# A Nystrom attention with an MLP on one core: another stationary operand for the iteration, late stores, and loads in parts

## The chip, the cores and the metric

One core of one Trainium2 chip. The metric is the time of one execution in device microseconds (us). Every kernel here was profiled once and timed in several rounds beside the kernel before on the same chip. Engines: PE is TensorE, DVE is VectorE, ACT is ScalarE, POOL is GpSimd, SP is the engine whose queue issues nearly all DMAs.

## The reference, cut to what matters

```python
# q, k, v: 8 batches, 8 heads, 576 rows, 64 columns; m = 32 landmarks (means of 18 rows)
A  = softmax(q    @ k_lm.T)          # 576 x 32 per head
Bm = softmax(q_lm @ k_lm.T)          # 32 x 32
C  = softmax(q_lm @ k.T)             # 32 x 576
Z  = Bm.T / (norm1(Bm) * norminf(Bm))
for _ in range(6):
    Z = 2 * Z - Z @ Bm @ Z           # inverse of Bm by iteration
attn = A @ Z @ C @ v
# then, over 4608 rows of 512: layer norm, MLP 512 -> 2048 -> 512 with relu, residual
```

## The kernel before: the parts that the change touches

Heads are handled four at a time, one above the other on 128 partitions; such a group of four is a unit (W units at once: two for one batch, four for two). The kernel does not iterate on Z. It holds E = (scaled Bm times its transpose) in the first 32 columns of a tile st and X, which starts as C @ v, in the other 64, and takes both from one product: E becomes 2E - EE and X becomes 2X - EX. Names that come up later: psn is that product in PSUM, ebd (fbd after the change) E (F) as a block-diagonal stationary operand; bmbd and zcbd are block-diagonal operands of the end of an attention, rcv the reciprocals that scale X; nat, asum and s are POOL's casts and sums for the landmarks; psh is the first product of the MLP and ot an output block.

```python
    def diagonal(name, src, W, mask):       # 32x32 blocks of four heads -> block diagonal 128x128
        t = asm.tile([P, W, 4, LM], FP16, name=name, tag=name, bufs=1)
        dve.tensor_tensor(out=t[:], in0=src[:, :, None, :].broadcast_to([P, W, 4, LM]),
                          in1=mask, op=ALU.mult)
        return t
    ...
        for it in range(6):
            lo = 0 if it < 5 else LM
            psn = p1([P, W, LM + D], "psn")
            for w in range(W):
                MM(psn[:, w, lo:], ebd[:, w, :, :].rearrange("p a l -> p (a l)"), st[:, w, lo:])
            stn = asm.tile([P, W, LM + D], FP16, name="st", tag="st")
            dve.scalar_tensor_tensor(out=stn[:, :, lo:], in0=st[:, :, lo:], scalar=2.0,
                                           in1=psn[:, :, lo:], op0=ALU.mult,
                                           op1=ALU.subtract)
            st = stn
            if it < 5:
                ebd = diagonal("ebd", st[:, :, 0:LM], W, masks(W))
            ...
```

The MLP is a stream of TensorE work, cut into 36 row blocks in nine groups; after each step of an attention, `fill(n)` puts n of its matmuls into the program. TensorE's order is thereby fixed. A group of the MLP needs the normalized rows (xn, by POOL) of four blocks, turned by DMA transposes (xnT). Batch 0 runs first with nothing to fill in but idle matmuls, then batch 1, batch 2, batches 3 and 4, 5 and 6, 7.

The softmax here doesn't subtract the row's maximum and nothing guards it: scores larger than these inputs give would overflow.

## Time and profile before

| | before |
|---|---|
| time, median of the first 3 runs | 329.13 us (328.23 to 330.18) |
| span of the profiled run | 327.9 us |
| TensorE busy | 314.7 us, 96% |
| first psh (start of the MLP) | 25.95 us |
| first psh of the fourth MLP group | 141.71 us |
| from there to the end | 186.2 us |

The prediction below shows the page's shares and slices. Two groups of instructions belong beside them; the columns are line, engine, operation, what it writes and reads with partitions and elements, count, then busy us, mean ns of one, and idle time of the engine before them with its cause.

```profile
L68 DVE SCALAR_TENSOR_TENSOR st<-st,psn 128x192 f16<-128x192 f16 (+3 forms) x36 | 14.2, 395 | 17.6 <-PE psn L74 17.4
L68 DVE TENSOR_TENSOR ebd<-st,mask 128x256 f16<-128x256 f16 (+1 forms) x30 | 20.7, 690 | 1.0
```

These are the two VectorE operations of each step. The reader is to see that the step is short, some 1 us of VectorE, and that ebd is the dearer half.

### The profile page before, as it was taken

The numbers are of one execution on the slowest core, as the hardware profiler recorded it, in microseconds if no ns is written. First come the engines' busy times: TensorE is split into PE (matmuls) and PEld (weight loads), VectorE is DVE, ScalarE is ACT, GpSimd is POOL, SyncE is SP. The second block draws the span as 40 slices with busy tenths as digits, with TensorE's granted clock in tenths as the row PEclk, the third lists the DMA queues.
The fourth block names the chain that finished last, engine by engine and source line by source line (L and its number), as shares of the span: only waits on it lengthen the run. The fifth ranks groups of instructions, "written<-read, shape, count | busy, mean of one in ns | idle before, by whom it ended". The sixth has DMA issues, their size and how long they took to land.

```text
span 327.9 us, 8249 instructions
## 1 busy us (share of the span) xinstructions
PE 314.7 (96%) x3409; PEld 162.3 (50%) x3409; DVE 175.7 (54%) x395; ACT 152.7 (47%) x307; POOL 153.3 (47%) x241
## 2 busy tenths in 40 slices
PE   8889999999999999989999999999999999999995
PEld 8547864553445444435544445454444444444444
DVE  3668769779964797953237668722566120010012
ACT  3546762749960661957204672454046107305600
POOL 3389979999999999999800034100014000000000
PEclk9999999999999999999999999999999999999998
DMA  7999999898797864695022103330242126032023
GB/s 278 394 356 365 366 402 303 297 345 239 241 195 231 234 169 127 156 290 102 4 68 66 34 20 76 82 50 2 64 104 26 32 64 98 0 72 60 0 49 79
DMA packets 36397, 50.34 MB, mean 154 GB/s; under 512 B 17796, under 2 KB 22152, under 8 KB 36360
## 3 DMA queue, kind: packets, MB, share of 16 engines
q1 hardware_dynamic: 36200, 49.69, 52.7%
q8 instruction: 26, 0.43, 0.5%
q10 hardware_dynamic: 160, 0.13, 0.2%
q14 instruction: 11, 0.09, 0.1%
HBM read 36.70 MB, written 9.44 MB: 141 GB/s over the span
## 4 chain that ended last, share of the span: by engine, by line
PE 56%; POOL 22%; DMA 7%; issue 2%; ACT 2%; DVE 1%; SPq 0%; POOLq 0%
PE psh L74 26%; PE pso L74 25%; POOL asum L68 11%; POOL nat L68 6%; POOL natv L68 3%; DMA stg<-in_q_dram 3%; POOL xn L68 2%; DMA w2stg<-in_moe_w_ch_dram 2%; POOL s L68 1%; PE psy L74 1%; PE pscv L74 1%; DMA stg<-in_v_dram 1%; DMA stg<-in_k_dram 1%; DMA xnT<-xn 1%; ACT xn L68 1%
## 5 line engine op out<-in xcount | busy, mean ns | idle before, releaser
L74 PE MATMUL psh<-xnT,w 128*128 128x512 f16 (+1 forms) x640 | 133.7, 358 | 1.4 <-DMA xnT<-xn 1.4
L74 PE MATMUL pso<-w,hT 128*128 128x512 f16 (+1 forms) x592 | 132.9, 374 | 0.0
L68 ACT ACTIVATE hT<-psh 128x512 f16<-128x512 f32 x144 | 84.9, 597 | 97.6 <-PE psh L74 97.4
L74 PEld LDWEIGHTS <-w 128*128 128x128 f16 x640 | 59.5, 98 | 56.7 <-issue 3.1
L74 PEld LDWEIGHTS <-hT 128*128 128x128 f16 x592 | 56.1, 98 | 57.2 <-issue 0.8
L68 DVE SCALAR_TENSOR_TENSOR ot<-pso,rstd,xblk 128x512 f32<-128x512 f32 (+1 forms) x37 | 27.1, 732 | 77.6 <-PE pso L74 77.4
L68 POOL CAST nat<-stg 128x1152 f16<-128x1152 f32 x28 | 32.5, 1167 | 3.4 <-DMA stg<-in_k_dram 1.7
L68 POOL TENSOR_TENSOR asum<-asum 128x256 f32<-128x256 f32 (+2 forms) x54 | 28.4, 527 | 4.2
L68 DVE TENSOR_TENSOR xblk<-psy,rcpd 128x512 f32<-128x512 f32 (+1 forms) x40 | 27.6, 691 | 1.8 <-POOL w L68 0.2
L68 POOL TENSOR_TENSOR asum<-nat 128x576 f32<-128x576 f16 x18 | 23.4, 1299 | 1.5
L68 POOL TENSOR_SCALAR xn<-xblk,mvg 128x512 f16<-128x512 f32 x14 | 9.6, 694 | 30.9 <-ACT junk L68 30.9
L68 DVE SCALAR_TENSOR_TENSOR st<-st,psn 128x192 f16<-128x192 f16 (+3 forms) x36 | 14.2, 395 | 17.6 <-PE psn L74 17.4
L68 POOL CAST natv<-stg 128x1152 f16<-128x1152 f32 (+1 forms) x16 | 17.6, 1119 | 9.6 <-DMA stg<-in_v_dram 9.6
L68 POOL TENSOR_SCALAR negm<-mvg 128x1 f32<-128x1 f32 x14 | 2.7, 191 | 40.5 <-DVE mvg L68 35.9
L68 DVE TENSOR_TENSOR ebd<-st,mask 128x256 f16<-128x256 f16 (+1 forms) x30 | 20.7, 690 | 1.0
L68 DVE STREAM_TRANSPOSE xT<-nat 128x576 uint32<-128x576 uint32 x24 | 18.2, 760 | 2.2 <-POOL nat L68 2.2
L74 PE MATMUL psy<-zcbd,ea 128*128 128x260 f16 (+1 forms) x80 | 15.9, 276 | 1.0 <-DVE xblk L68 0.4
L68 ACT ACTIVATE ea<-psea 128x576 f16<-128x576 f32 x12 | 7.2, 648 | 16.5 <-PE psea L74 16.5
L74 PE MATMUL idle<-zeros 128*128 128x128 f16 (+2 forms) x82 | 13.4, 312 | 1.1 <-DVE eps_ln L172 1.1
L74 PEld LDWEIGHTS <-ea 128*128 128x128 f16 (+1 forms) x80 | 7.1, 100 | 12.2 <-issue 3.5
L68 ACT ACTIVATE junk<-xblk 128x512 f16<-128x512 f32 x14 | 8.8, 625 | 9.4 <-DVE xblk L68 9.2
L68 DVE BATCH_NORM_STATS2 st<-xblk 128x6 f32<-128x512 f32 x18 | 12.4, 688 | 0.5
(115 smaller groups left out, 263.0 us busy)
## 6 DMA issues: line engine op xcount, KB each, us to landing
stg<-in_q_dram SPq DMA_DIRECT2D x16, 576.0 KB, 6.0
stg<-in_k_dram SPq DMA_DIRECT2D x16, 576.0 KB, 5.7
out_dram<-ot SPq DMA_DIRECT2D x70, 128.0 KB, 2.4
stg<-in_v_dram SPq DMA_DIRECT2D x10, 576.0 KB, 6.4
w1stg<-in_moe_w_ch_dram SPq DMA_DIRECT2D x16, 256.0 KB, 6.0
w2stg<-in_moe_w_ch_dram SPq DMA_DIRECT2D x16, 256.0 KB, 5.2
stg<-in_v_dram SPq DMA_DIRECT2D x12, 288.0 KB, 5.5
xnT<-xn SPq DMA_TRANSPOSE x28, 3.3
```

The source lines that it names most:

```text
L68: return lambda *args, **kw: keep(getattr(self.engine, op)(*args, **kw))
L74: keep(nc.tensor.matmul(o, l, r, start=start, stop=stop, tile_position=(rb, cb), skip_group_check=(skip or cb != 0)))
```

## The change

Its intent: shorten a step. With F = 2 - E as stationary operand, F times (E, X) is already the next (E, X), so VectorE has only to copy psn to st, and the next F can be taken straight from psn, without reading st. Off-diagonal blocks of fbd stay 0 for good, so only the four diagonal blocks are written, one op each. Beside it: stores of the output are put into the queue one step later, behind the loads and transposes of the step; the last loads of batch 0's k and v come in two parts; fewer idle matmuls there; bmbd is built before the iteration.

```diff
+    def two_less(e, W):
+        for h in range(4):
+            rows = ds(32 * h, 32)
+            dve.scalar_tensor_tensor(
+                out=fbd[rows, 0:W, h, :], in0=e[rows, :, :], scalar=-1.0,
+                in1=twos[rows, None, :].broadcast_to([32, W, LM]), op0=ALU.mult, op1=ALU.add)
+
+    def newton(st, psn, W, it):
+        if it < 5:
+            dve.tensor_copy(out=st[:], in_=psn[:])
+            two_less(psn[:, :, 0:LM], W)
+        else:
+            dve.tensor_copy(out=st[:, :, LM:], in_=psn[:, :, LM:])
 ...
-        ebd = diagonal("ebd", st[:, :, 0:LM], W, masks(W))
+        two_less(st[:, :, 0:LM], W)
 ...
-                MM(psn[:, w, lo:], ebd[:, w, :, :].rearrange("p a l -> p (a l)"), st[:, w, lo:])
+                MM(psn[:, w, lo:], fbd[:, w, :, :].rearrange("p a l -> p (a l)"), st[:, w, lo:])
-            dve.scalar_tensor_tensor(out=stn[:, :, lo:], in0=st[:, :, lo:], scalar=2.0, ...)
+            newton(stn, psn, W, it)
-            if it < 5:
-                ebd = diagonal("ebd", st[:, :, 0:LM], W, masks(W))
 ...
+        bmbd = asm.tile(...)          # now before the iteration
 ...
-                store(j, ot)
+                if at_end:
+                    store(j, ot)
+                else:
+                    to_store.append((j, ot))
 ...
+    def work(n):
+        k = len(to_store)
+        fill(n)
+        settle()
+        for _ in range(k):
+            store(*to_store.pop(0))
 ...   (k and v of batch 0 in parts, two warm-ups shortened: not shown)
```

The first `two_less` of each attention reads st, which lies in SBUF; the others read psn, which lies in PSUM. And each of its four ops starts on other partitions than the one before. (Batch 0 keeps its own form of the iteration.)

More of the change, by code (lines that the diff above doesn't have):

```diff
@@ L78, in TR, with load @@
         keep(nc.tensor.matmul(o, i_, idn, is_transpose=True, tile_position=(0, 0)))
-    def load(src, b, u, queue):
+    whole = ((slice(0, 2), slice(0, NJ)),)
+    halves = ((slice(0, 2), slice(0, 5)), (slice(0, 2), slice(5, NJ)))
+    pairs = ((slice(0, 1), slice(0, NJ)), (slice(1, 2), slice(0, NJ)))
+    def load(src, b, u, queue, parts=whole):
         t = stage.tile([P, 2, NJ, D], FP32, name="stg", tag="stg")
-        keep(queue.dma_start(
-            out=t[:],
-            in_=src[b, 4 * u:4 * u + 4].rearrange("(r e) (t j) d -> (e t) r j d", e=2, j=NJ)))
+        rows = src[b, 4 * u:4 * u + 4].rearrange("(r e) (t j) d -> r (e t) j d", e=2, j=NJ)
+        for r, j in parts:
+            keep(queue.dma_start(out=t[:, r, j, :],
+                                 in_=rows[r][:, :, j, :].rearrange("r p j d -> p r j d")))
         return t
@@ L92, in load_qk @@
             raw[b]["q", u] = load(q, b, u, nc.sync)
-            raw[b]["k", u] = load(k, b, u, nc.sync)
+            raw[b]["k", u] = load(k, b, u, nc.sync, halves if (b, u) == (0, U - 1) else whole)
     def load_v(b):
         for u in range(U):
-            raw[b]["v", u] = load(v, b, u, nc.sync)
+            raw[b]["v", u] = load(v, b, u, nc.sync, pairs if (b, u) == (0, U - 1) else whole)
     def load_seg(src, b, u, queue, turned=False):
@@ L111, in cast_qk @@
         t = nat.tile([P, NJ, 2, D], FP16, name="nat", tag="nat")
-        engine.tensor_copy(out=t[:].rearrange("p j r d -> p r j d"), in_=raw[b][nm, u][:])
+        for _, j in halves if (b, u, nm) == (0, U - 1, "k") else whole:
+            engine.tensor_copy(out=t[:, j, :, :].rearrange("p j r d -> p r j d"),
+                               in_=raw[b][nm, u][:, :, j, :])
         nat_tiles[b, nm, u] = t
@@ L165 @@
     maskw = const.tile([P, 4, 4], FP16, name="maskw")
-    mask16 = const.tile([P, 4], FP16, name="mask16")
-    nc.gpsimd.tensor_copy(out=mask16[:], in_=mask4[:])
+    fbd = const.tile([P, 4, 4, LM], FP16, name="fbd")
+    nc.gpsimd.memset(fbd[:], 0.0)
+    twos = const.tile([P, LM], FP16, name="twos")
+    for i in range(4):
+        nc.gpsimd.tensor_copy(out=twos[ds(32 * i, 32), :],
+                              in_=ident16[ds(32 * i, 32), ds(32 * i, 32)])
+    nc.gpsimd.tensor_tensor(out=twos[:], in0=twos[:], in1=twos[:], op=ALU.add)
     for w in range(4):
@@ L191 @@
     pool.tensor_copy(out=natv_buf[0][:, 2, :, 0:D], in_=raw[0]["v", 1][:, 0])
+    pool.tensor_copy(out=natv_buf[0][:, 3, 5:NJ, 0:D], in_=raw[0]["v", 1][:, 1, 5:NJ])
     bones = const.tile([P, 4, 32], FP16, name="bones")
@@ L279, in warm @@
             MM(idle[:, 0:cols], zeros[:], zeros[:, None, :].broadcast_to([P, cols // P, P]))
-    def diagonal(name, src, W, mask):
-        t = asm.tile([P, W, 4, LM], FP16, name=name, tag=name, bufs=1)
-        dve.tensor_tensor(out=t[:], in0=src[:, :, None, :].broadcast_to([P, W, 4, LM]),
-                          in1=mask, op=ALU.mult)
-        return t
-    def masks(W):
-        return mask16[:, None, :, None].broadcast_to([P, W, 4, LM])
+    def two_less(e, W):
[10 more added lines that the diff above has]
+            dve.tensor_copy(out=st[:, :, LM:], in_=psn[:, :, LM:])
     def attention(bs):
@@ L309, in attention, with sums @@
                 pst = p2([P, NJ, P], FP16, "pst")
-                def sums():
-                    for j in range(NJ):
+                def sums(js=range(NJ)):
+                    for j in js:
                         MM(pss[:, i, w, :], n16[:, j, :, :].rearrange("p r d -> p (r d)"),
@@ L316, in attention @@
                 last = (w, i) == (W - 1, 1)
-                if last:
+                if last and not first:
                     sums()
-                for j in range(NJ):
-                    TR(pst[:, j, :], n16[:, j, :, :].rearrange("p r d -> p (r d)"), ident16[:])
+                for js in (range(0, 5), range(5, NJ)) if first and last else (range(NJ),):
+                    if first and last:
+                        sums(js)
+                    for j in js:
+                        TR(pst[:, j, :], n16[:, j, :, :].rearrange("p r d -> p (r d)"),
+                           ident16[:])
                 t = aprep.tile([P, NJ, P], FP16, name="xT", tag="xT" + nm, bufs=5 if nm == "q" else 4)
@@ L325, in attention @@
                     scalar.copy(t[:], pst[:])
+                else:
+                    scalar.copy(t[:, 0:5, :], pst[:, 0:5, :])
                 xT[nm, w] = t
@@ L340, in attention @@
         if first:
-            dve.tensor_copy(out=t[:], in_=pst[:])
+            dve.tensor_copy(out=t[:, 5:NJ, :], in_=pst[:, 5:NJ, :])
         yield
@@ L378, in attention @@
         psse = psse_[:, 0:2, :].rearrange("p a (u l) -> p a u l", u=W)
+        MM(psse[:, 0, :, :], bones[:].rearrange("p a c -> p (a c)"), bm16[:])
         for w in range(W):
@@ L382, in attention @@
                 MM(psse[sl, 1, w, :], bmT[sl, w, :], bmT[sl, w, :], rb=32 * h, cb=32 * h)
-        MM(psse[:, 0, :, :], bones[:].rearrange("p a c -> p (a c)"), bm16[:])
         dve.tensor_reduce(out=psse_[:, 2, 0:W], in_=psse[:, 0, :, :], axis=AX.X,
@@ L401, in attention @@
             natv = natv_of[b]
-            for j in range(NJ):
-                for h in range(4):
-                    r, e = divmod(h, 2)
-                    rows = ds(64 * e, 64)
-                    MM(pscv[ds(32 * h, 32), w, :], ect[w][rows, j, ds(32 * r, 32)],
-                       natv[rows, 2 * u + r, j, :], rb=64 * e, cb=32 * h,
-                       start=(j == 0), stop=(j == NJ - 1), skip=True)
+            order = [(j, h) for j in range(NJ) for h in range(4)]
+            if first and w == W - 1:
+                order.sort(key=lambda jh: jh[1] // 2)
+            for j, h in order:
+                r, e = divmod(h, 2)
+                rows = ds(64 * e, 64)
+                MM(pscv[ds(32 * h, 32), w, :], ect[w][rows, j, ds(32 * r, 32)],
+                   natv[rows, 2 * u + r, j, :], rb=64 * e, cb=32 * h,
+                   start=(j == 0), stop=(j == NJ - 1), skip=True)
         rcv = asm.tile([P, W], FP32, name="rcv", tag="rcv")
@@ L426, in attention @@
                 else:
-                    MM(psn[:, w, lo:], ebd[:, w, :, :].rearrange("p a l -> p (a l)"),
+                    MM(psn[:, w, lo:], fbd[:, w, :, :].rearrange("p a l -> p (a l)"),
                        st[:, w, lo:])
             stn = asm.tile([P, W, LM + D], FP16, name="st", tag="st")
-            dve.scalar_tensor_tensor(out=stn[:, :, lo:], in0=st[:, :, lo:], scalar=2.0,
-                                           in1=psn[:, :, lo:], op0=ALU.mult,
-                                           op1=ALU.subtract)
+            if first:
+                dve.scalar_tensor_tensor(out=stn[:, :, lo:], in0=st[:, :, lo:], scalar=2.0,
+                                         in1=psn[:, :, lo:], op0=ALU.mult, op1=ALU.subtract)
+            else:
+                newton(stn, psn, W, it)
             st = stn
-            if not first and it < 5:
-                ebd = diagonal("ebd", st[:, :, 0:LM], W, masks(W))
             if it < W:
@@ L658, in attention2 @@
                                 op=ALU.mult)
-        ebd = diagonal("ebd", st[:, :, 0:LM], W, masks(W))
+        two_less(st[:, :, 0:LM], W)
         pscv = ps2.tile([P, 2, 512], FP32, name="pscv", tag="p2")
@@ L679, in attention2 @@
         v_used.update(c.bs)
+        bmbd = asm.tile([P, W, 4, LM], FP16, name="bmbd", tag="bmbd", bufs=1)
+        dve.tensor_tensor(out=bmbd[:], in0=bm16[:, :, None, :].broadcast_to([P, W, 4, LM]),
+                          in1=maskw[:, 0:W, :, None].broadcast_to([P, W, 4, LM]), op=ALU.mult)
         pcv = pscv[:, :, 0:(W // 2) * (D + 1)].rearrange("p x (y e) -> p y x e", e=D + 1)
@@ L695, in attention2 @@
             for w in range(W):
-                MM(psn[:, w, lo:], ebd[:, w, :, :].rearrange("p a l -> p (a l)"), st[:, w, lo:])
+                MM(psn[:, w, lo:], fbd[:, w, :, :].rearrange("p a l -> p (a l)"), st[:, w, lo:])
             stn = asm.tile([P, W, LM + D], FP16, name="st", tag="st")
-            dve.scalar_tensor_tensor(out=stn[:, :, lo:], in0=st[:, :, lo:], scalar=2.0,
-                                           in1=psn[:, :, lo:], op0=ALU.mult,
-                                           op1=ALU.subtract)
+            newton(stn, psn, W, it)
             st = stn
-            if it < 5:
-                ebd = diagonal("ebd", st[:, :, 0:LM], W, masks(W))
-            else:
-                bmbd = diagonal("bmbd", bm16, W,
-                                maskw[:, 0:W, :, None].broadcast_to([P, W, 4, LM]))
             if it < W // 2:
@@ L940, in mlp @@
                                          in1=x_blk.pop(j)[:], op0=ALU.mult, op1=ALU.add)
-                store(j, ot)
+                if at_end:
+                    store(j, ot)
+                else:
+                    to_store.append((j, ot))
                 yield True
     stream = mlp()
+    to_store, at_end = [], []
     def fill(n):
@@ L958 @@
     warm(50, 128)
-    for _ in range(4):
+    for i in range(4):
         run(a0)
-        warm(3, 256)
+        if i < 3:
+            warm(3, 256)
     run(a0)
-    warm(1, 512)
+    warm(1, 128)
     run(a0)
-    scalar.copy(natv_buf[0][:, 3, :, 0:D], raw[0]["v", 1][:, 1])
+    scalar.copy(natv_buf[0][:, 3, 0:5, 0:D], raw[0]["v", 1][:, 1, 0:5])
     warm(1, 512)
@@ L1038 @@
     for i, _ in enumerate(a1):
-        fill(5 if i < 9 else 7)
-        settle()
+        work(5 if i < 9 else 7)
         next_cast()
@@ L1053 @@
         for step, _ in enumerate(attention2(c.bs, c)):
-            fill(count[step])
-            settle()
+            work(count[step])
             if late and step >= 3:
@@ L1063 @@
         while after and (after.jobs or after.lms):
-            fill(8)
+            work(8)
             next_cast()
             after.next_job()
+    at_end.append(True)
     for _ in stream:
-        pass
+        while to_store:
+            store(*to_store.pop(0))
 _INS = ['q', 'k', 'v', 'moe_g_ln', 'moe_w_ch1', 'moe_w_ch2']
```

## The prediction

> **What bounds the kernel now**
>
> I read the page's busy shares and slices first, then TensorE's order of work for its gaps, then VectorE's order of work where those gaps lie, then the DMA queue.
>
> ```profile
> PE 314.7 (96%) x3409; PEld 162.3 (50%) x3409; DVE 175.7 (54%) x395; ACT 152.7 (47%) x307; POOL 153.3 (47%) x241
> ...
> PE   8889999999999999989999999999999999999995
> ...
> DVE  3668769779964797953237668722566120010012
> ...
> POOL 3389979999999999999800034100014000000000
> ```
>
> TensorE (PE) is the bound: 327.9 - 314.7 leaves 13.2 us idle in the span, nearly all in the first half. No more than that is to be won, because the change removes no matmul of the MLP or the attention. POOL is full from slice 7 to 17 (about 50 to 142 us), VectorE (DVE) nearly full in some of these slices. TensorE's order of work is fixed by the program, with a fixed number of MLP matmuls between two steps of an attention; where that number is too small for the VectorE work of a step, TensorE stalls. Its gaps, from its order of work:
>
> ```profile
> 49.03 0.23 PE L74 MATMUL psn<-st,ebd 128*128 128x64 f16 x2 [0.26 <-DVE ebd L68]
> ...
> 77.12 0.26 PE L74 MATMUL psn<-st,ebd 128*128 128x96 f16 x2 [0.60 <-DVE ebd L68]
> ...
> 120.37 0.34 PE L74 MATMUL psn<-st,ebd 128*128 128x96 f16 x4 [0.70 <-DVE ebd L68]
> ...
> 141.71 1.89 PE L74 MATMUL psh<-xnT,w 128*128 128x512 f16 x8 [1.42 <-DMA xnT<-xn]
> ```
>
> I compared the starts of neighbouring groups with 0.216 us per 512-column matmul (64 of them take 13.81 us in the chain that ended last). By that measure about 6 us are lost between 26 and 142 us, and after 142 us nothing to speak of. The gaps at psn are VectorE's st and ebd; the largest is a DMA transpose. VectorE's order of work beside them:
>
> ```profile
> 45.37 0.35 DVE L68 SCALAR_TENSOR_TENSOR st<-st,psn 128x192 f16<-128x192 f16 x1 [0.41 <-PE psn L74]
> 45.76 0.42 DVE L68 TENSOR_TENSOR ebd<-st,mask 128x256 f16<-128x256 f16 x1
> ...
> 117.99 0.55 DVE L68 SCALAR_TENSOR_TENSOR st<-st,psn 128x384 f16<-128x384 f16 x1
> 118.58 1.74 DVE L68 TENSOR_TENSOR ebd<-st,mask 128x512 f16<-128x512 f16 x1
> ```
>
> The same ebd of two units (four) takes 0.42 (0.69) us when POOL is out of the way and up to 0.93 (1.74) when not. The gap at 141.71 is seen in the order of work around it:
>
> ```profile
> 135.75 1.20 SPq L870 DMA_TRANSPOSE xnT<-xn  x1
> 137.04 1.24 SPq L829 DMA_DIRECT2D out_dram<-ot  x2
> 138.38 1.25 SPq L870 DMA_TRANSPOSE xnT<-xn  x1
> ```
>
> The two stores stand in the queue between two transposes. The last xn was ready by 136.2, its transpose was issued at 138.38 and landed about 3.2 us later.
>
> Last, the first 26 us, a latency chain with idle matmuls as filler:
>
> ```profile
> 10.22 0.43 PE L74 MATMUL pss<-pm,nat 128*128 128x64 f16 x9 [0.25 <-DVE nat L68]
> ...
> 14.24 0.47 PE L74 MATMUL pscv<-natv,ect 64*32 64x65 f16 x36 [0.31 <-POOL natv L68]
> ```
>
> The reader is to see that the first attention waits once for k's last cast and once for v's; v's last part lands at about 13.45.
>
> **What the Trainium skill says**
>
> "SBUF — State Buffer", section "SBUF: two separate sides": GpSimd and VectorE share one port pair under an exclusive lock, and a VectorE op with two SBUF inputs takes it. The trace agrees: ebd has two SBUF inputs and stretches from 0.69 to 1.74 us, while st<-st,psn, with one input from PSUM, stays within 0.51 to 0.56.
> "VectorE: DVE Perf Modes", section "Why PSUM operands drop a tier": fp32 from PSUM runs at one element per cycle. Agrees: klm<-pss, a cast of 128 elements from PSUM, takes 288 ns, zcbd with 256 takes 412.
> Same page, section "Two Vector instructions with no wait between them": an op whose operand starts in another quadrant of 32 partitions than the last is held until all earlier ones have finished. This trace hardly shows it: after an xblk of 64 rows (129.63, 0.69 us) the next op starts 0.73 us later, after one of 128 rows (132.40, 0.69 us) 0.61 us later; the first may also have waited for something else. "Four heads in turn" means a new quadrant each time.
>
> **The change part by part**
>
> *Start.* k's last part comes in two loads and is cast, summed and turned in halves. Its last cast then takes 4/9 of 0.76 = 0.34 us, so sums end some 0.5 us sooner, and three idle matmuls of 256 columns and most of one of 512 go (0.5 us): psb starts about 0.8 us sooner than 11.64. But v's last half still lands at 13.45, since the DMA engines are full there. The whole of it is cast in 0.68 us now, in 4/9 by POOL and 5/9 by ACT later, about 0.4 us; and with its matmuls sorted last, only 18 of them follow. So rcv comes at about 14.3 in place of 14.76. I take 0.5 us off; the steps of that attention after it are unchanged. The order of the two psse products is hidden.
>
> *Iteration.* Before: st (0.35 us for two units, 0.55 for four), 0.04 us, ebd (0.42 or 0.69, more when contended). Added: a copy psn to st of the same size (by the rows above 0.35 and 0.55, starts of the next op 0.29 and 0.49 on, as overlap of unheld ops in the trace is about 0.07) and four small ops from PSUM of 64 or 128 elements. st<-st,psn takes 264 ns for 128 elements and 348 for 192, so I estimate 0.20 for 64. Held, with 0.03 us between: 0.29 + 3 x 0.23 + 0.20 = 1.18 us against 0.35 + 0.04 + 0.42 = 0.81 free of contention (1.3 at worst); for four units 0.49 + 3 x 0.295 + 0.264 = 1.64 against 1.28 free (2.3 at worst). So the step from psn to the next psn becomes longer by about 0.36 us where there was no contention and shorter where there was. The path is not less work; it is work that POOL cannot stretch. Laid on the order of work, VectorE's other jobs kept in place:
> - attention of batch 1, 41 to 50 us: the first op set has two SBUF inputs, +0.35 (0.9 for 0.54). The first two steps are filled for 1.64 us by matmuls, 0.29 + 1.18 + 0.06 = 1.53 fits: 0. The next two were 1.18 each: +0.35 each. The last was 1.59 by contention: -0.06. Together +1.0.
> - batch 2, 70 to 84: filled for 1.6, with a transpose (0.7) or reduce (1.3) of VectorE in each step. The two contended steps come out even, the next two +0.36 each; at the end bmbd (1.16 contended, now earlier) is off the path: -0.4. Together about +0.35.
> - batches 3 and 4, 110 to 125: the contended steps (1.37, 1.74) save what the others lose: 0.
> - batches 5 and 6, 170 to 187: one step of four has VectorE behind it: +0.35. Batch 7: filled, 0.
> Sum +1.7 us. VectorE's busy time rises by some 10 us (about 20.7 us of ebd go, 15 x 4 x 0.2 + 12 x 4 x 0.27 and the first sets come), which by itself bounds nothing.
>
> *Late stores.* They leave the queue to the transposes and loads. The transpose of 138.38 can go at 137.0, landing 1.3 us sooner, so the gap of 1.42 at 141.71 goes. But this is a meeting of two: TensorE would have been there at 140.2; with -0.5 and +1.35 it comes at about 141.05, transpose landed: 0.7 us sooner than now. The stores' own time is hidden; those at the end stay where they are.
>
> Sum: 141.7 becomes 141.0, then +0.35 in batches 5 and 6: about -0.4 us, 328.7 against 329.1.
>
> **The rivals**
>
> *Small ops overlap or are cheaper.* If four ops in other quadrants start as close as unheld ones (0.07 + 64 elements at 0.96 GHz, 0.13 us), a step costs 0.29 + 3 x 0.13 + 0.2 = 0.9 us, near 0.81, and every contended step is won: TensorE gets to 142 us some 2.5 us sooner, POOL too without ebd in its way, until the transposes of POOL's xn bound it. About 326. For it: the change was written for a tuned kernel, its author knew the costs. Against: the rule of the skill. I give it a good third.
>
> *Small ops are dearer,* 0.26 and 0.33 each: by the same laying out +5.5 us in the attentions, of which 1.4 are absorbed at 141.7: 332 to 333. For it: psum reads of 64 elements in the tensor_tensor form took 0.225. A sixth.
>
> *POOL bounds.* It is full from 50 to 142 and its xn feeds the transposes. Then any gain before 142 us would be lost again at the first psh of the fourth group. It caps the first rival at about -3 us.
>
> **Range and chances**
>
> The working gives 328.7; weighting the rivals (326 more probable than 332.5) I say 328.0, range 325.3 to 330.9. Faster by over 2% needs 322.5, about half of all TensorE idle time: 0.05. Slower by over 2% needs 335.7, more than the dear case: 0.02. Within 2%: 0.93.
>
> **What would show it**
>
> Start right: rcv's first op near 14.3, first psh near 25.5. Iteration right: four small ops in turn of 0.2 and 0.26 us, each starting after the last has ended, psn to psn in batch 1 about 1.5 us; wrong if they overlap. Stores right: no store between the transposes before the fourth group's first psh, and that wait under 0.3 us. POOL's share: no asum stretched beside the small ops. The prediction fails if TensorE's idle time changes by over 3 us, or if a gap opens after 142 us.

## The result, and the profile after

The changed kernel takes 334.11 us (median of 6, 333.15 to 335.59) against 329.38 us of the kernel before (median of 6). The ratio is 1.0148, with a 95% interval of 1.0117 to 1.0179. Here and below a ratio is the mean time of one kernel's fast runs over that of the other's of the same rounds, so not quite the ratio of the medians. It is slower by 1.5%: 328.0 was predicted, with a range up to 330.9.

| us | before | after |
|---|---|---|
| span of the profiled run | 327.9 | 331.8 |
| first psh | 25.95 | 25.78 |
| first psh of the fourth group | 141.71 | 145.50 |
| from there to the end | 186.2 | 186.3 |

So 3.8 of the span's 3.9 us are there by 146 us, all of them from after 26 us; after 146 us hardly anything changes. The page of the changed kernel, shares, slices, and three groups of it:

```profile
PE 315.3 (95%) x3406; PEld 163.1 (49%) x3406; DVE 193.6 (58%) x486; ACT 153.5 (46%) x308; POOL 152.4 (46%) x247
...
PE   8889979987899998999999999999999999999995
...
DVE  3568879899987899874447758832767020020012
...
L68 DVE SCALAR_TENSOR_TENSOR fbd<-psn,twos 32x64 f16<-32x64 f32 (+1 forms) x100 | 24.5, 245 | 2.5
...
L74 PE MATMUL psn<-st,fbd 128*128 128x96 f16 (+1 forms) x84 | 8.4, 206 | 7.8 <-DVE fbd L68 4.5
...
L68 DVE SCALAR_TENSOR_TENSOR fbd<-st,twos 32x64 f16<-32x64 f16 (+1 forms) x20 | 12.7, 635 | 0.4
```

TensorE's work is the same, its idle time 3.3 us more. VectorE is busy 17.9 us longer. An op of the form fbd<-psn takes 245 ns on average; the same op from st, of the same size, takes 635 ns. TensorE's order of work has these waits (start, duration, in brackets the idle time before and what ended it):

```profile
43.19 0.26 PE L74 MATMUL psn<-st,fbd 128*128 128x96 f16 x2 [1.67 <-DVE st L68]
...
48.26 0.26 PE L74 MATMUL psn<-st,fbd 128*128 128x96 f16 x2 [0.37 <-DVE fbd L68]
...
75.49 0.24 PE L74 MATMUL psn<-st,fbd 128*128 128x96 f16 x2 [1.60 <-DVE st L68]
...
82.63 0.26 PE L74 MATMUL psn<-st,fbd 128*128 128x96 f16 x2 [0.88 <-DVE fbd L68]
...
128.58 0.29 PE L74 MATMUL psn<-st,fbd 128*128 128x64 f16 x4 [0.57 <-DVE fbd L68]
...
145.50 1.89 PE L74 MATMUL psh<-xnT,w 128*128 128x512 f16 x8
```

Two kinds of loss are seen: a wait of about 1.6 us at the first psn of batch 1 and of batch 2, and waits of 0.4 to 0.9 us at the steps. The wait for the transpose at the fourth group is gone. Counted as lost time at psn by the prediction's own measure (starts of neighbouring groups less 0.216 us per 512-column matmul), batch 1 went from 0.7 to 3.5 us, batch 2 from 0.8 to 4.4, batches 3 and 4 stayed at 1.5, batches 5 and 6 went from 0 to 0.4.

VectorE's order of work in batch 1:

```profile
40.61 2.00 DVE L68 SCALAR_TENSOR_TENSOR fbd<-st,twos 32x64 f16<-32x64 f16 x4
...
46.84 0.36 DVE L68 CAST st<-psn 128x192 f16<-128x192 f32 x1 [0.35 <-PE psn L74]
47.23 0.97 DVE L68 SCALAR_TENSOR_TENSOR fbd<-psn,twos 32x64 f16<-32x64 f32 x4
```

A step is copy plus four ops, 0.39 + 0.97 us, where st and ebd took 0.39 + 0.42 free of contention. From psn to psn it is 1.71 us (46.55, 48.26, 49.98), where it was 1.18. The first set takes 2.00 us. In batch 2 it is worse; VectorE and POOL, from the order of work of both:

```profile
68.10 1.14 POOL L68 CAST nat<-stg 128x1152 f16<-128x1152 f32 x1
...
68.48 3.53 DVE L68 SCALAR_TENSOR_TENSOR fbd<-st,twos 32x64 f16<-32x64 f16 x4
69.32 1.27 POOL L68 TENSOR_TENSOR asum<-nat 128x576 f32<-128x576 f16 x1
...
70.67 1.65 POOL L68 TENSOR_TENSOR asum<-asum 128x256 f32<-128x256 f32 x3
```

Four ops of 0.2 us take 3.53 us while POOL works through three instructions and more: each small op waits for POOL anew. In narrow windows of the trace the four end at 69.31, 70.67, 71.48 and 72.01, each under 0.1 us after the end of a POOL instruction (69.24, 70.59, 71.39, 71.93), and each of the last three starts within 0.02 us of POOL's next one. ot, a transpose, bmbd and rcv stand behind them in VectorE's order, and so TensorE gets its first psn 1.6 us late.

### The profile page after: what moved, and what is told of

Read it like the earlier page. It is cut to its first block, busy times and chain, and to the rows that moved or that the text cites. A ratio compares the mean times of both kernels' runs of the same rounds, so it can differ in the third digit from the quotient of the medians.

```text
span 331.8 us, 8341 instructions
## 1 busy us (share of the span) xinstructions
PE 315.3 (95%) x3406; PEld 163.1 (49%) x3406; DVE 193.6 (58%) x486; ACT 153.5 (46%) x308; POOL 152.4 (46%) x247
## 4 chain that ended last, share of the span: by engine, by line
PE 72%; DVE 13%; DMA 7%; POOL 3%; ACT 2%; issue 2%; SPq 1%; POOLq 0%
PE pso L74 34%; PE psh L74 30%; DVE fbd L68 5%; DMA w1stg<-in_moe_w_ch_dram 4%; DMA stg<-in_v_dram 3%; DVE xT L68 2%; PE psy L74 2%; PE pscv L74 2%; DVE st L68 2%; POOL asum L68 2%; ACT xn L68 1%; SPq L90 1%; DVE ot L68 1%; PE psn L74 1%; PE psea L74 1%
## 5 line engine op out<-in xcount | busy, mean ns | idle before, releaser
L68 POOL TENSOR_TENSOR asum<-asum 128x256 f32<-128x256 f32 (+2 forms) x54 | 27.0, 500 | 4.2
L68 DVE SCALAR_TENSOR_TENSOR fbd<-psn,twos 32x64 f16<-32x64 f32 (+1 forms) x100 | 24.5, 245 | 2.5
L68 POOL CAST natv<-stg 128x1152 f16<-128x1152 f32 (+2 forms) x17 | 17.9, 1076 | 7.0 <-DMA stg<-in_v_dram 7.0
L68 DVE CAST st<-psn 128x192 f16<-128x192 f32 (+3 forms) x30 | 12.6, 420 | 11.2 <-PE psn L74 10.4
L74 PE MATMUL psn<-st,fbd 128*128 128x96 f16 (+1 forms) x84 | 8.4, 206 | 7.8 <-DVE fbd L68 4.5
L74 PEld LDWEIGHTS <-fbd 128*128 128x128 f16 x84 | 5.6, 97 | 17.2 <-DVE fbd L68 9.9
L68 DVE SCALAR_TENSOR_TENSOR fbd<-st,twos 32x64 f16<-32x64 f16 (+1 forms) x20 | 12.7, 635 | 0.4
```

The source lines that it names most:

```text
L68: return lambda *args, **kw: keep(getattr(self.engine, op)(*args, **kw))
L74: keep(nc.tensor.matmul(o, l, r, start=start, stop=stop, tile_position=(rb, cb), skip_group_check=(skip or cb != 0)))
```

## The experiments

Theory: the loss is the iteration's, in two parts, the first sets (two SBUF inputs, held by POOL, four times) and the steps (four ops that do not overlap). Rivals: the late stores or the split loads cost it; or one of the two parts alone.

### e1_old_iter: the change without its iteration

```diff
-        two_less(st[:, :, 0:LM], W)
+        ebd = diagonal("ebd", st[:, :, 0:LM], W, masks(W))
-            newton(stn, psn, W, it)
+            (st, ebd and bmbd as in the kernel before; late stores and split loads stay)
```

> Late stores and split loads of the change, with the iteration of before put back. Theory (the whole loss lies in the new iteration; the other parts gain): first psh 0.2 us sooner, the wait of 1.4 us for the transpose at the fourth group's first psh gone: some 1.5 us less than before, ratio 0.993 to 0.998. Rival (the late stores or the extra loads hurt, by buffers or the queue's order): ratio 1.003 or more.

Measured: 328.96 us, ratio 0.999 (0.997 to 1.0011). So the other parts cost nothing, and the whole loss is the iteration's (with the place of bmbd, for which see e7). But they give next to nothing either, against my expectation. The queue around the fourth group:

```profile
136.22 1.20 SPq L885 DMA_TRANSPOSE xnT<-xn  x1
137.47 0.60 SPq L841 DMA_DIRECT2D out_dram<-ot  x1
138.16 1.27 SPq L885 DMA_TRANSPOSE xnT<-xn  x1
...
141.75 1.89 PE L74 MATMUL psh<-xnT,w 128*128 128x512 f16 x8 [1.00 <-DMA xnT<-xn]
```

One of the two store instructions still stands between the transposes. It is the second half of one block's output, whose ot was written at 130.82 and whose first half went out at 131.59; the program pins the order of transposes and loads in the queue, but not that of the stores, and why this one was placed there I have not followed up. The gain in the queue is 0.6 us, not 1.3; the last transpose is issued at 138.16, against 138.38, because POOL came 0.46 us later to its xn in this run (135.32 against 134.86). From issue to the first psh it then takes 3.6 us where it took 3.3. TensorE waits 1.00 us where it waited 1.42.

### e2_old_iter_stores_early: split loads alone

```diff
-                if at_end:
-                    store(j, ot)
-                else:
-                    to_store.append((j, ot))
+                store(j, ot)          # on top of e1
```

> Split loads alone: iteration and stores of before put back. Theory: only the 0.17 us at the first psh are left and they are lost again at the transpose that the fourth group waits for: ratio 0.998 to 1.001, that wait 1.3 to 1.7 us. If the late stores do nothing this run equals the one with late stores.

Measured: 329.01 us, ratio 0.999 (0.9975 to 1.0006); the wait for the transpose is 0.84 us, less than I expected. With and without late stores the time is the same. The split loads are not shown to be worth anything: the first psh comes at 25.73 here, at 26.03 in e1, at 25.78 in the changed kernel, and at 26.40 in e4, with the same start of the program in all four and a full clock up to there. That spread is larger than the gain of 0.5 us that I had predicted from them.

### e3_first_from_psum: the first set also from PSUM

```diff
-        dve.tensor_tensor(out=st[:, :, 0:LM], in0=psse[:, 1, :, :], in1=cinv..., op=ALU.mult)
-        two_less(st[:, :, 0:LM], W)
+        dve.tensor_tensor(out=psse[:, 1, :, :], in0=psse[:, 1, :, :], in1=cinv..., op=ALU.mult)
+        dve.tensor_copy(out=st[:, :, 0:LM], in_=psse[:, 1, :, :])
+        two_less(psse[:, 1, :, :], W)
```

> The changed kernel, but the first stationary operand of each attention is also written from PSUM (the product is put back into its PSUM tile, one copy added), so that no op of the new set has two SBUF inputs. Theory (of the loss of about 4.7 us some 3 lie in the first sets, whose small ops each wait for a POOL instruction): small ops 0.2 to 0.3 us each, the waits of 1.67 and 1.60 us at the first psn of batches 1 and 2 down to under 0.5, time about 331, ratio 1.004 to 1.008. Rival (the loss is the length of each step): ratio 1.012 or more.

Measured: 331.12 us, ratio 1.0056 (1.0037 to 1.0074), as expected. VectorE in batch 1, and the psn after it:

```profile
41.42 0.91 DVE L68 SCALAR_TENSOR_TENSOR fbd<-psse,twos 32x64 f16<-32x64 f32 x4
```

```profile
42.92 0.26 PE L74 MATMUL psn<-st,fbd 128*128 128x96 f16 x2 [0.73 <-DVE st L68]
```

The set takes 0.91 us in place of 2.00, and on average one of its ops of 64 elements takes 218 ns where it took 526. The wait at the first psn of batch 1 falls from 1.67 to 0.73 us, less far than expected, that of batch 2 disappears. In ratios the first sets cost 1.0148 - 1.0056 = 0.0092, 3.0 us of 329.4, though the two ratios are from different rounds. The rest of the loss, 0.0056 or 1.8 us, is left to the steps by subtraction.

### e4_after_stores_early: the changed kernel with its stores early

The edit is that of e2, on the changed kernel.

> The changed kernel with its stores put back where they were. Theory: TensorE comes some 3 us later to the fourth group, so the transpose is there anyway and the order of the stores is worth under 0.4 us: ratio 1.014 to 1.017. Rival (late stores are worth their 1.4 us in the changed kernel too): 1.018 or more.

Measured: 334.95 us, ratio 1.0168 (1.0147 to 1.019); the interval overlaps that of the changed kernel. Three of its four runs have a mean clock of 0.995 (see e9); the fourth, at 1.0, took 334.2 us, where the changed kernel's four runs at 0.998 and more took 333.15 to 334.30. No wait for the transpose is left here, although two stores stand between the transposes again: TensorE comes so late that the transpose has landed. So TensorE's lateness alone is enough to remove the wait of 1.42 us; the late stores are not needed for it.

### e5_one_op and e6_one_quadrant: what makes the four ops long

Their outputs are wrong, which doesn't matter for the times. e5 writes one block with all 128 partitions; e6 writes all four blocks from partitions 0 to 31.

```diff
-        for h in range(4):
-            rows = ds(32 * h, 32)
-            dve.scalar_tensor_tensor(out=fbd[rows, 0:W, h, :], in0=e[rows, :, :], scalar=-1.0, ...)
+        dve.scalar_tensor_tensor(out=fbd[:, 0:W, 0, :], in0=e, scalar=0.0, ...)      # e5
```
```diff
-            rows = ds(32 * h, 32)
+            rows = ds(0, 32)                                                          # e6
```

> The changed kernel with one small op of 128 partitions in place of the four in turn (the result is wrong on purpose: only one block is written; the scalar is 0 so that nothing grows). Theory (the steps lose by the length of four ops one after the other): psn to psn in batch 1 falls from 1.71 to about 1.0 to 1.2 us, the waits of 0.37 to 0.88 us for the small ops go, and of the first sets only one wait for POOL each is left: some 4 to 5.5 us less than the changed kernel, ratio 0.997 to 1.003. Rival (the copy or the matmuls of the new form cost the time): 1.010 or more.

> The changed kernel with all four small ops on partitions 0 to 31 (wrong result on purpose), so that none starts in another quadrant than the one before. If the change of quadrant holds each op until the last has ended: starts 0.12 to 0.16 us apart for 64 elements (0.245 in the changed kernel) and 0.19 to 0.22 for 128 (0.31), psn to psn in batch 1 about 1.35, ratio 1.004 to 1.009. If the ops simply take that long in a row: spacing and time as in the changed kernel, ratio 1.013 to 1.016.

Measured: e5 326.29 us, ratio 0.9901 (0.9878 to 0.9924); e6 326.48 us, ratio 0.9908 (0.9886 to 0.993). Both gain more than expected, 25 and 24 thousandths of the time before, against the changed kernel, and end faster than the kernel before. VectorE in batch 1 of e6, to be held against 46.84 and 47.23 of the changed kernel:

```profile
46.13 0.36 DVE L68 CAST st<-psn 128x192 f16<-128x192 f32 x1 [0.77 <-PE psn L74]
46.40 0.59 DVE L68 SCALAR_TENSOR_TENSOR fbd<-psn,twos 32x64 f16<-32x64 f32 x4
```

The first sets of batches 1 and 2 in e6, against 40.61 and 68.48 of the changed kernel:

```profile
40.64 1.45 DVE L68 SCALAR_TENSOR_TENSOR fbd<-st,twos 32x64 f16<-32x64 f16 x4
...
66.01 1.22 DVE L68 SCALAR_TENSOR_TENSOR fbd<-st,twos 32x64 f16<-32x64 f16 x4
```

The same number of ops of the same shape on the same engine: 0.59 us in place of 0.97. With the last op's 0.20 taken off, three starts lie (0.59 - 0.20) / 3 = 0.13 us apart; in the changed kernel (0.97 - 0.22) / 3 = 0.25. The first op also starts 0.27 us after the copy and not 0.39. That is the rule of held ops that the prediction cites from the Trainium skill: an op that starts in another quadrant than the last is held until all earlier ones have ended. A wait for a semaphore between the ops is ruled out in the first sets: there the second and the third op carry none in either trace, yet in the changed kernel they start 0.02 us after the one before has ended (69.31, 69.33), in e6 before it has (the first runs from 40.64 to 41.27, the second starts at 41.20). The rule even covers the first op of a set in batch 1: the last op that read SBUF before it was the previous set's fourth (twos, on partitions 96 to 127), and so it is held behind the copy; in batch 2, where a transpose of full height lies between, the changed kernel starts it 0.26 us after the copy (76.61, 76.87). Psn to psn is 1.21 us (45.84, 47.05). e6 also shortens the first sets, from 2.00 to 1.45 and from 3.53 to 1.22 us, which is why it gained more than I expected from the hold in the steps alone. So the two causes do not look independent: in the changed kernel's set of batch 2 POOL has the lock before each held op, while of e6's only every second one waits (about 0.6 and 0.2 us in turn in batch 1). e5, with one op, is no faster than e6: it waits 0.85 us for the fourth group's transpose, e6 for none. That speaks for a floor near 326 us.

### e7_old_iter_bmbd: bmbd early, with the iteration of before

The edit moves bmbd before the iteration, on top of e1.

> The run with the iteration of before, late stores and split loads, but bmbd built before the iteration as in the change. Theory: the wait of 0.3 to 0.4 us for zcbd at the end of batch 2 goes, but the fourth group's transposes, which hang on POOL, take it back: ratio 0.997 to 1.0. If TensorE's waits before that point counted in full: 0.996 or less.

Measured: 329.8 us, ratio 1.001 (0.9988 to 1.0031); no gain. The wait for zcbd went, but in its profiled run ebd of two units took 693 ns on average, against 548 in the kernel before, and TensorE lost 6.8 us at psn against 2.9 in e1: I take it that any change ahead shifts how POOL's and VectorE's instructions meet; no run isolates this.

### e8_mask_psum: the old iteration, masks in PSUM

ebd has two SBUF inputs, st and the mask. Here the mask is copied once into an unused corner of a PSUM bank, as is that of bmbd; apart from the small PSUM tiles becoming views of one bank (they shared one buffer before, too) nothing else differs from e7.

```diff
+    bank = ps1.tile([P, 512], FP32, name="bank", tag="p1")
+    mask_ps = bank[:, 448:452]
+    maskw_ps = bank[:, 456:472].rearrange("p (w h) -> p w h", w=4)
+    scalar.copy(mask_ps, mask4[:])
+    scalar.copy(maskw_ps, maskw[:])
 ...   (the small PSUM tiles of the attentions become views of bank's first 448 columns)
-        return mask16[:, None, :, None].broadcast_to([P, W, 4, LM])
+        return mask_ps[:, None, :, None].broadcast_to([P, W, 4, LM])
```

> As the last, and the masks of ebd and bmbd lie in PSUM, so that ebd has one SBUF input. Theory (ebd is stretched by POOL through its second SBUF input, and stretches POOL): every ebd 0.42 to 0.50 (two units) and 0.69 to 0.78 us (four), psn waits for ebd under 0.3 us each, POOL's work before the fourth group 1 to 2 us sooner: ratio 0.990 to 0.996. Rival (nothing before the fourth group counts, or the read from PSUM is dearer): 0.998 or more.

Measured: 325.72 us, ratio 0.9887 (0.9866 to 0.9909), correct, and a little better than expected. Groups of VectorE by shape, and the queue with the fourth group's first psh:

```profile
L68 DVE TENSOR_TENSOR ebd<-st,bank 128x512 f16<-128x512 f16 x12 | 8.2, 686 | 0.4
L68 DVE TENSOR_TENSOR ebd<-st,bank 128x256 f16<-128x256 f16 x18 | 7.6, 420 | 0.6
```

```profile
132.15 1.19 SPq L901 DMA_TRANSPOSE xnT<-xn  x1
133.40 0.61 SPq L857 DMA_DIRECT2D out_dram<-ot  x1
134.10 1.24 SPq L901 DMA_TRANSPOSE xnT<-xn  x1
...
137.93 1.89 PE L74 MATMUL psh<-xnT,w 128*128 128x512 f16 x8 [0.94 <-DMA xnT<-xn]
```

Every ebd now takes 0.42 or 0.69 us, none is stretched, and the read from PSUM costs nothing: the SBUF form took the same when POOL was out of the way. POOL gains as well: its asum ops from nat take 1271 to 1282 ns, where they took up to 1603, and s, which took up to 750, stays within 322; its last xn before the fourth group starts at about 131.9, in the kernel before at 135.5. The fourth group starts at 137.93, and the end follows 185.9 us later. It still waits 0.94 us for the transpose.

### e9_steps_one_quadrant: only the steps without the hold

As e6, but the first set of each attention stays as the change has it (wrong result).

```diff
-    def two_less(e, W):
+    def two_less(e, W, same=False):
-            rows = ds(32 * h, 32)
+            rows = ds(0 if same else 32 * h, 32)
-            two_less(psn[:, :, 0:LM], W)
+            two_less(psn[:, :, 0:LM], W, same=True)
```

> The changed kernel, with the four small ops of each step on partitions 0 to 31 (wrong result on purpose), the first set of each attention left as the change has it (four quadrants, two SBUF inputs). Theory (steps and first sets both lose): the waits for the small ops within the steps go (a sum of some 6 us at psn), those of 1.6 to 1.9 us at the first psn of batches 1 and 2 stay, so the time lies between the run with all small ops in one quadrant (0.991) and the changed kernel (1.0148): ratio 0.997 to 1.005. If the first sets alone were the loss: 1.012 or more.

Measured: 328.74 us (median of six, one of which, 331.89, is slow); ratio of the fast runs 0.9956 (0.9916 to 0.9996), a little below what I expected. The waits of 2.20 and 1.44 us at the first psn of batches 1 and 2 stand, those within the steps for fbd are gone. So both parts of the theory are real: undone alone, the first sets give 3.0 us (e3) and the steps' hold about 1.0148 - 0.9956 = 0.0192, 6 us, with a good 1 us of doubt. They do not add up: e6, which takes the hold from both, gains 0.0240.

The spread of the fast runs (326.19 to 329.97) goes with TensorE's clock: 326.19 and 326.98 had a mean clock of 0.998 and 1.0, the three slower ones 0.995. By the former two alone the ratio would be 0.991, and the steps' hold worth nearly 8 us. In the profiled run the clock is 0.57 from 45 to 49 us, after the wait of 2.20 us, and in that of e4 0.58 from 44 to 48, after a wait of 2.04. Mean clocks of 0.995 and less occur in e4, e9 and two of the six runs of the changed kernel (0.995 and 0.993), and in no run of another kernel. Long first sets may thus cost time in this way too; that the wait brings the lower clock about is not shown.

### e10_before_mask, e11_mask_stores_early, e12_mask_rcv: what of e8 counts

e10 is the kernel before with the masks in PSUM and nothing else. e11 is e8 with its stores early, by the edit of e2. e12 is e8 with one more op freed of its second SBUF input:

```diff
-        dve.reciprocal(out=rcv_, in_=pcv[:, :, :, D])
-        dve.tensor_tensor(out=rcv[:], in0=rcv[:], in1=cinv[:], op=ALU.mult)
+        rcv_ps = bank[:, 480:480 + W]
+        dve.reciprocal(out=rcv_ps..., in_=pcv[:, :, :, D])
+        dve.tensor_tensor(out=rcv[:], in0=rcv_ps, in1=cinv[:], op=ALU.mult)
```

> The kernel before with nothing but the masks of ebd and bmbd in PSUM. Theory (the masks alone give the gain of the last run but one; late stores, split loads and early bmbd add little): ratio 0.987 to 0.992. Rival (the gain needs the other parts of the change): 0.993 or more.

> The run with masks in PSUM, late stores and split loads, but the stores put back where they were. There TensorE waits 0.9 us for the transposes of the fourth group even with late stores. If the late stores help once TensorE is early, this is slower by 0.5 to 1.2 us than with them, ratio about 0.991 to 0.993; if they do nothing, 0.988 to 0.990.

> The same run with late stores, and the reciprocal that is multiplied with cinv also written to PSUM, so that this op too has one SBUF input. It is 0.16 us alone and up to 1.1 us beside POOL. Theory: the wait of 0.49 us at the first psn of batch 2 shrinks, but the transposes that the fourth group waits for take it back: ratio 0.987 to 0.990, not faster than the run without it by more than 0.3 us.

Measured: e10 326.55 us, ratio 0.9905 (0.987 to 0.9939); e11 325.76 us, ratio 0.9887 (0.9862 to 0.9911); e12 325.54 us, ratio 0.9885 (0.9859 to 0.9911). All three are correct. The masks alone give the gain; whether the rest adds to it lies within the intervals. Late stores do nothing here either: e8 and e11 have the same ratio and waits of 0.94 and 0.95 us for the transpose. In e12 the wait at batch 2's first psn is gone, and the wait for the transpose has grown to 1.42 us: what TensorE gains before the fourth group it now waits for there.

## Why the prediction was wrong

- *What bounds the kernel, and that only the time before 142 us counts:* right. In all of the profiled runs 185.8 to 186.4 us follow the fourth group's first psh; that start alone decides the time (137.93 in e8, 146.95 in e4).
- *Iteration, "Sum +1.7 us":* this is the step that failed. At psn batch 1 lost 2.8 us more than before (+1.0 predicted) and batch 2 3.6 us more, of which bmbd's earlier place gave back some 0.5 at the end (+0.35 predicted for both together). Its two terms that were mis-sized:
  - The first op set was put at +0.35 us in batch 1 and has no term in batch 2. It cost +1.6 and +1.8 by the lost time at the first psn. Its 0.9 us is the length of four held ops that wait for nobody (3 x 0.23 + 0.20), though the text says itself that this set has two SBUF inputs and had read the lock from ebd; each of the four has to get the lock for itself, and on average 0.2 us of work became 0.5 us in batch 1 and 0.9 in batch 2. In batch 2 TensorE had work before the first psn, but VectorE's other ops of that stretch stand behind the set. e3 takes this part away and recovers 3.0 us.
  - A step from psn to psn was put at 1.53 us in batch 1 and is 1.71: the ops lie 0.245 apart (0.23 predicted), and the copy does not overlap the first of them (0.39 for 0.29). Over batches 1 and 2 the steps cost +1.2 and +1.9 us, where the same laying out had +0.64 and +0.72. In batches 3 and 4 (0) and 5 and 6 (+0.4) the predicted terms held.
  - VectorE's busy time was to rise by some 10 us, with 12 x 4 ops of 128 elements where the program has 10 x 4; it rose by 17.9, since the first sets alone take 12.7.
- *Held ops:* right, and shown by e6 (0.25 us from start to start, 0.13 without the hold). That a hold also lets POOL in between two ops of a first set was not in the prediction.
- *Late stores, "that gap goes":* it went, but for another reason. One store instruction stays between the transposes (e1), and the last transpose then takes longer to land; TensorE came later, and that alone removes the gap (e4). That the term came true is luck. Late stores were worth nothing measurable in three pairs: e1 and e2, e8 and e11, and the changed kernel and e4, whose intervals overlap.
- *Start, -0.5 us:* 0.17 in the profiled run, and within what one run differs from the other. v's wait ended at 14.15, against 14.24.
- *Rivals:* the one I gave a sixth, "small ops are dearer", came nearest, with 332 to 333, but by luck: it had ops of 0.26 and 0.33 us, measured are 0.22 and 0.28, and most of the loss has other causes. The one I gave a good third, because the author must know the costs, was an argument about the author and not about the profile. "POOL bounds" was right as a cap: e5, e8, e10, e11 and e12 all wait for the fourth group's transpose, 0.78 to 1.42 us, and in e8 POOL works without a pause up to the xn that this transpose turns.
- *Signs:* the prediction was to fail if TensorE's idle time changed by over 3 us, and it changed by 3.3. The sign for the stores, no store between the transposes, did not come either: one is issued at 139.55, between transposes at 138.16 and 140.24.

What stays open: why a transpose that is issued sooner after the last one takes longer to its first use (3.8 us in e8, 3.4 in e11, 3.3 before; in e1, e8 and e12 the transpose before it takes 4.7 to 5.0 us to land, and it lands under 1 us behind that one, so it may be waiting for it), and how much of the gain of e8 over e10 is real. The best version measured is e8, with e11 and e12 alike: 1.1% faster than the kernel before and, from two ratios of different rounds, about 2.6% faster than the change.

## What to carry to other kernels

Replacing one wide VectorE op by several narrow ones saved elements here, not time. Each pays a fixed part (0.219 us for 64 elements, 0.284 for 128: by these, an estimated 0.15 us of either), and one op on all 128 partitions took no longer (0.214 us in e5). In another quadrant an op did not overlap the one before, and with two SBUF inputs and the hold each could wait for GpSimd again. When a VectorE op is stretched by GpSimd, look first for the operand that can live in PSUM; here two masks of 80 bytes per partition together were worth more than the rewriting of the iteration. And before counting a gain, find the next meeting point of the engines (here one group's transposes) and ask how much of the gain is let through.

## What the Trainium skill lacked or had wrong

- "SBUF — State Buffer", section "SBUF: two separate sides": the exclusive lock is as the page says (e8: ebd 0.69 us always, where it reached 1.74). It gives the lock to one instruction at a time; it lacks what that means for a row of small ops, four of which, of 0.22 us, took 3.53 us beside POOL, and does not name the way out that worked here, a small constant operand moved to PSUM (a ratio of 0.9905 in e10).
- "VectorE: DVE Perf Modes": the hold that the prediction cites from it is right, but has no cost there; here it is 0.25 us from start to start against 0.13, for ops of 64 elements from PSUM. Its section "The perf-mode tier table (the rule you actually need)" has tensor_tensor twice as fast from SBUF in 16 bits as from PSUM. The table alone can mislead: here the mask in PSUM cost nothing, 0.42 and 0.69 us in both places, and 256 more elements take 0.27 us, about one per ns, so this op did not run in the faster mode from SBUF either. The condition stands elsewhere on the page (a step of one element), and the mask is broadcast along its last dimension.
- "DMA: Bandwidth & Descriptors", section "DMA Transpose (X-bar)": no figure for transposes of 128x512 that follow each other closely. Issued 2.6 us after the last one, it took 3.3 us to its first use (kernel before), issued 1.95 us after it 3.6 to 4.0 us (e1, e8, e12).
